# One-core attention-plus-MLP layer: values stored in 64-column groups, a reordered start, and a different cut of the last output tile

## Chip, core and metric

The kernel runs on one core of one Trainium2 chip. The metric is the device time of one execution in microseconds (us). The kernel before takes 269.57 us, the median of three runs (269.50 to 269.68).

The engines are named as in the profile: PE is the matrix engine, PEld its weight loads, DVE the vector engine, ACT the scalar (activation) engine, POOL the general-purpose vector engine, SP the engine whose queue issues most DMAs. PE writes to PSUM (8 banks of 512 f32 columns); the other operands lie in SBUF.

## What is computed

For x of 2048 tokens by 640 features (cut to what matters):

```python
xn = layernorm(x)                                  # per token, eps 1e-5
q, k, v = split(xn @ wqkv)                         # 32 heads of 20
phi(t) = concat(softmax(t @ w_phi), softmax(-(t @ w_phi)))   # 40 features a head
kv = einsum("sf,sd->fd", phi(k), v); z = phi(k).sum(0)       # per head
attn = (phi(q) @ kv) / (phi(q) @ z + 1e-6)         # linear attention
out = x + attn @ wo + (silu(xn @ w1) * (xn @ w3)) @ w2       # F = 1536
```

## The kernel before

**Tiles.** The tokens are 16 tiles of 128 rows (`T`). A tile is normalized in place in `x_tok`, transposed into `xnT` (features on partitions, 5 chunks of 128), and all projections take `xnT` from there. Tiles 0 to 3 are transposed on PE (`xn_transpose`, 5 transposes each, then a copy from PSUM by ACT or DVE); the later ones by DMA transposes.

**Stages, as PE sees them.** (1) Warm-up matmuls on zeros (`idle`, `warm_up`), the transposes of tiles 0 to 3 and their value projections (`v_part`: two halves q of 320 columns, 5 matmuls each, then one copy to `v2` on ACT, `v_store`). (2) The first MLP chunks (`mlp`: 10 matmuls of 512 columns for one chunk of 128 hidden features and 512 tokens) and `fold_mm`, which folds `w_phi` into the key and query weights. (3) Keys and values tile by tile (`k_tile`, `v_tile`). ACT takes exponentials into `ekt`, DVE sums them, POOL divides (`k_norm`, two POOL instructions a tile). (4) `kv_sum`: for each tile 11 groups of three heads, one matmul a group, 63 moving columns (3 heads of 20 values and a one), 42 in the last group, accumulated over the 16 tiles in PSUM. (5) Queries (`q_proj` to `q_tok`), with MLP chunks as filling. `q_tok` has 11 matmuls of 63 columns a tile as well, whose moving operand `KVc` lies in groups of 64 columns. (6) The remaining MLP chunks and the outputs, `out_tile`: 17 chunks accumulate into a 128 by 640 result, DVE adds x, a DMA on SP's queue stores it.

**Values.** `v2` holds, for each tile, 32 heads of 21 bf16 columns (20 values and a one), 672 columns in all. Group g of `kv_sum` starts at column 63 g, that is at byte 126 g of the tile's 1344 bytes. The ones are written by one POOL memset in `consts_late`.

**The order.** The order on each engine is not written out: `_Program` records operations, and a planner at the end of the kernel asks 14 streams (`norms`, `transposes`, `fold_k`, `attention`, `k_norms`, ...) for their next step and commits the one that can start first by a cost model. A stream holds back with `yield None` until counters in `done` are reached. Dependencies are found by granules of SBUF, `GRAN` = 32 bytes (line 23): two operations that touch one granule are ordered, on the same engine too (the second waits for the first one's semaphore). PSUM is tracked by bank.

**The start.** `first_loads` issues on SP and ACT: x tile 0 in two halves, x tile 1, x tile 2, the two halves of the value weights `wv`, x tile 3, then MLP weights. The statistics of tiles 0, 2 and 3 are two `bn_stats` (`ln_half`), a `bn_aggr`, an add of eps on DVE and a power of -1/2 on POOL (`ln_rstd`). Those of tile 1 are two sums by ACT with the mean, eps step and power in between (`act_sum`, `scalar_op`, `act_rstd`). `ln_apply` normalizes on DVE. `norms` gives the order of all this.

**The end.** Tile 15's output is made in two column parts, 0 to 384 and 384 to 640, each with 17 matmuls, one DVE addition and one DMA on SP's queue, so that the first part's addition and store run beside the second part's matmuls (lines 699 to 706).

Of the kernel before, what the change touches and what calls it, by code (L numbers as in the profile page):

```python
# [9 lines left out]
D = 640  # L10
# [9 lines left out]
DEN_EPS = 1e-6  # L20

ENGINES = ("PE", "ACT", "DVE", "POOL", "SP")
GRAN = 32


def heads_of_chunk(c):
# [223 lines left out]
def bass_parallel_sum__linear_kernel_hedgehog__glu_gated_swiglu__prompt_kernel(  # L250
# [11 lines left out]
    bf = DT.bfloat16  # L262
    LAG = 4.0
    QLEAD = 2
    IDLE1, IDLE2 = 11, 8
    f32 = DT.float32
    P = _Program(nc)

# [18 lines left out]
    GM = new("GM", [128, DC, H], bf)  # L287
    phi_s = new("phi_s", [128, DC, DH], bf)
    BDc = new("BDc", [128, DC, 8 * DH], bf)
    bst = new("bst", [128, T, 16], f32)  # L290
    mv = new("mv", [128, T, 8], f32)
    rstd = new("rstd", [128, T, 8], f32)
    mhalf = new("mhalf", [128, 4], f32)
    warm = new("warm", [128, 8], f32)
    M3 = new("M3", [128, 4], bf)
# [28 lines left out]
    eqT = [new(f"eqT{i}", [128, NG, 128], bf, (RKV, RE + 27648)[i // 2] + 5632 + 2816 * (i % 2)) for i in range(4)]  # L324
    hT = [hT0, hT1, hT2, hT3]

    RV = region(21504)
    v2 = new("v2", [128, T, H * 21], bf, RV)
    oT = new("oT", [128, DC, S], bf, RV)

    RW = region(12800)
# [59 lines left out]
    def memset(eng, o, v):  # L391
        P.op(eng, "memset", [o], [], (o, v), cost=0.15 + free(o) / 960)
# [52 lines left out]
    def consts_late():  # L445
        memset("POOL", M3[:, 0:3], 1.0)
        select(M3[:, 0:3], 0, [[-40, 3]], 1, ALU.is_ge, 0.0)
        select(M3[:, 0:3], 40, [[40, 3]], -1, ALU.is_gt, 0.0)
        memset("POOL", ekt[:, T * 2 * D:T * 2 * D + 48], 1.0)
        memset("POOL", v2[:].rearrange("p t (h c) -> p t h c", c=21)[:, :, :, DH], 1.0)  # L450


    def ln_half(t, q):
        i, o = x_tok[:, t, 320 * q:320 * q + 320], bst[:, t, 6 * q:6 * q + 6]
# [49 lines left out]
                 cost=0.9)  # L504

    def warm_up():
        idle(7, 512)
        idle(IDLE1, 128)

    def idle(n, cols):  # L510
        z = t1[:, 2, :]
        for _ in range(n):
            mm(bank(7, cols), z[:, 0:128], z[:, 0:cols], True, True, cost=cols / 1200)

    def xn_transpose(t, k):
        dst = xnT[:, :, t * 128:(t + 1) * 128]
# [30 lines left out]
        evac(dst[:, dc, :].rearrange("p (b c) -> p b c", c=320), bank2(k, 320))  # L547


    def proj(t, w, k):  # L550
        for q in range(2):
            for i in range(DC):
                mm(bank(k + q, 320), xnT[:, i, t * 128:(t + 1) * 128],
                   w[:, i, 320 * q:320 * q + 320], i == 0, i == DC - 1)

    def v_part(t, q, i, k):
        mm(bank(k + q, 320), xnT[:, i, t * 128:(t + 1) * 128], wv[:, i, 320 * q:320 * q + 320],
           i == 0, i == DC - 1)

    def v_store(t, k):  # L560
        pv = bank2(k, 320).rearrange("p b (h c) -> p b h c", c=DH)
        act(v2[:, t, :].rearrange("p (b h c) -> p b h c", b=2, c=21)[:, :, :, 0:DH], pv, ACT.Copy)

    def v_tile(t, k):
        proj(t, wv, k)
        v_store(t, k)

    def k_tile(t, k):
# [15 lines left out]
    def group(g):  # L584
        return 3 * g, min(3, H - 3 * g)

    def at_group(k, g, n):
        return bank(k + g // 8, n, 64 * (g % 8))

    def kv_sum(t0, t1, k):  # L590
        for t in range(t0, t1):
            for g in range(NG):
                h, nh = group(g)
                w = t * 2 * D + 120 * g
                mm(at_group(k, g, 21 * nh), ekt[:, w:w + 128], v2[:, t, 21 * h:21 * (h + nh)],
                   t == 0 and g % 8 == 0, t == T - 1 and g in (7, NG - 1), True, 0.03)

    def kv_store(k):
# [94 lines left out]
    def out_tile(t, k):  # L693
        b, ti = divmod(t, 4)
        if t + 2 < T:
            load_xres(t + 2)
        chunks = [(oT[:, i, t * 128:(t + 1) * 128], wo_s, i) for i in range(DC)]
        chunks += [(hT[b][:, i, ti * 128:(ti + 1) * 128], w2_s, i) for i in range(FC)]
        if t == T - 1:
            for q, lo, hi in ((0, 0, 384), (1, 384, D)):  # L700
                for n, (l, w, i) in enumerate(chunks):
                    mm(bank(k + q, hi - lo), l, w[:, i, lo:hi], n == 0, n == len(chunks) - 1)
                r = xres[:, t % 4, lo:hi]
                tt("DVE", r, bank(k + q, hi - lo), r, ALU.add)
# [19 lines left out]
    done = dict.fromkeys(("w", "ln", "t", "f", "k", "n", "kv", "v", "u", "qp", "qn", "qd", "q", "o", "h"), 0)  # L724

    def norms():
        yield lambda: (first_loads(), consts())
        yield lambda: act_sum(1, ACT.Copy, bst[:, 1, 0:1])
        yield lambda: (ln_half(0, 0), ln_half(0, 1), ln_rstd(0, 1))
        yield lambda: scalar_op(1, mv[:, 1, 0:1], bst[:, 1, 0:1], -1.0 / D, 0.0)  # L730
        yield lambda: act_sum(1, ACT.Square, mv[:, 1, 1:2], mv[:, 1, 0:1])
        yield lambda: ln_apply(0)
        done["ln"] = 1
        yield lambda: act_rstd(1)
        yield lambda: ln_half(2, 0)
        while done["t"] < 1:
# [12 lines left out]
        todo = []  # L749
        for t in range(4, T + 2, 2):  # L750
            if t == T or t > done["k"] + 8:
                for u in todo:
                    yield lambda u=u: ln_apply(u)
                    done["ln"] = u + 1
                todo = []
            if t == T:
                break
            while t > done["k"] + 8:
                yield None
            yield lambda t=t: ln_stats(t, 2)  # L760
# [47 lines left out]
    def attention():  # L808
        def v(t):
            return lambda: v_tile(t, banks(2))  # L810

        yield warm_up
        for t in range(4):
            while done["t"] <= t:
                yield None
            k = banks(2)
            held.add(k // 2)
            for q in range(2):
                for i in range(DC):
                    yield lambda t=t, q=q, i=i, k=k: v_part(t, q, i, k)  # L820
# [197 lines left out]
```

## Time and profile before

| | |
|---|---|
| median of three runs | 269.57 us |
| the profiled execution | 269.42 us |
| its span, first to last instruction | 267.7 us |
| PE busy | 262.3 us, 98% |
| DVE, POOL, ACT busy | 171.3, 103.0, 99.5 us |
| granted PE clock | 1.0 |

Times within the profile count from the start of the span. A row of the timeline gives start, duration, engine, line, operation, output<-input, shape and how many instructions are merged (x5); in brackets is the idle time of the engine before and what ended it. A matmul's duration contains its way through the array, so that matmuls overlap: how fast PE works is read from the distance of their starts, that is (duration of the row - duration of one matmul) / (count - 1). A few matmul records are missing from a trace (here 464 of 480 of one kind): a hole that is just one matmul wide is such a record and no stall. Most operations have line 102, the helper that records them, so tiles tell them apart. The DMA view gives, for each issue, the median time from issue to landing.

### The profile page before, as it was taken

The page shows a single profiled execution, that of the slowest core. Times are in us where ns is not written, and L with a number is a line of the kernel's source. Part 1 is how long each engine was busy: PE and PEld are TensorE (multiplying, and loading weights), DVE is VectorE, ACT ScalarE, POOL GpSimd, SP SyncE. Part 2 cuts the span into 40 slices and gives each one's busy share as a digit, 9 for nine tenths or more (in the row PEclk, how much of TensorE's full clock was granted, in tenths as well). Part 3 has the DMA queues.
Part 4 walks back from the last instruction along what each step waited for, and adds up shares of the span by engine and source line. Part 5 has one row for each costly group of instructions (what it writes and reads, how often), then busy time and mean ns, then how long its engine had stood idle before and what let it go on. Part 6 is the DMA issues. An engine that isn't in the chain of part 4 may idle for free.

```text
span 267.7 us, 4797 instructions
## 1 busy us (share of the span) xinstructions
PE 262.3 (98%) x1943; PEld 160.9 (60%) x1962; DVE 171.3 (64%) x292; ACT 99.5 (37%) x193; POOL 103.0 (38%) x144
## 2 busy tenths in 40 slices
PE   7999999999999999999999999999999999999996
PEld 4656677776745545554455455444577777777774
DVE  4559899998886878888888887898512121212112
ACT  5557979988324443334442344322100000000000
POOL 4316748999996364444444444420000000000000
PEclk9999999999999999999999999999999999999999
DMA  7998695900093444555474464214212213131301
GB/s 223 279 322 155 148 220 109 309 12 2 2 326 73 78 78 81 97 100 95 78 88 95 78 82 78 44 38 78 49 51 74 75 55 94 51 98 49 95 30 49
DMA packets 63510, 27.73 MB, mean 104 GB/s; under 512 B 49792, under 2 KB 63488, under 8 KB 63488
## 3 DMA queue, kind: packets, MB, share of 16 engines
q1 hardware_dynamic: 62688, 26.94, 43.4%
q10 hardware_dynamic: 800, 0.49, 0.6%
q8 instruction: 15, 0.25, 0.4%
q14 instruction: 7, 0.06, 0.1%
HBM read 12.81 MB, written 2.62 MB: 58 GB/s over the span
## 4 chain that ended last, share of the span: by engine, by line
PE 96%; DMA 1%; ACT 1%; issue 1%; DVE 0%; POOL 0%; SPq 0%
PE PS L102 96%; DMA x_tok<-in_A_x_dram 1%; ACT t L102 1%; POOL rstd L102 0%; DVE x_tok L102 0%; DVE xres L102 0%; SPq L114 0%; DVE rstd L102 0%; DVE mv L102 0%
## 5 line engine op out<-in xcount | busy, mean ns | idle before, releaser
L102 PE MATMUL PS<-xnT,w_s 128*128 128x512 bf16 x464 | 105.7, 379 | 1.0 <-ACT Wkp L102 0.2
L102 PEld LDWEIGHTS PS<-xnT,w_s 128*128 128x128 bf16 x480 | 45.8, 98 | 51.3 <-ACT Wkp L102 0.2
L102 PE MATMUL PS<-w_s,hT 128*128 128x320 bf16 (+2 forms) x384 | 54.9, 299 | 0.0
L102 DVE TENSOR_TENSOR xres<-PS,xres 128x640 bf16<-128x640 f32 (+2 forms) x17 | 13.4, 785 | 60.0 <-PE PS L102 60.0
L102 ACT ACTIVATE th<-PS 128x512 f32<-128x512 f32 x48 | 28.8, 600 | 49.0 <-PE PS L102 49.0
L102 PEld LDWEIGHTS PS<-w_s,hT 128*128 128x128 bf16 x384 | 37.6, 98 | 14.6
L102 DVE SCALAR_TENSOR_TENSOR t<-th,PS 128x512 bf16<-128x512 f32 x48 | 32.4, 675 | 20.8 <-ACT th L102 20.8
L102 POOL TENSOR_TENSOR ekt<-ekt,rS 128x640 bf16<-128x640 bf16 x32 | 39.5, 1277 | 0.6 <-DVE rS L102 0.6
L102 ACT ACTIVATE eq<-PS 128x600 bf16<-128x600 f32 (+1 forms) x72 | 24.7, 411 | 29.6 <-PE PS L102 29.5
L102 DVE SCALAR_TENSOR_TENSOR hT<-t,PS 128x512 bf16<-128x512 bf16 x48 | 33.0, 687 | 1.7
L102 PE MATMUL PS<-wv,xnT 128*128 128x320 bf16 x160 | 24.7, 299 | 0.1
L102 PE MATMUL PS<-wo_s,oT 128*128 128x320 bf16 (+2 forms) x160 | 24.5, 299 | 0.0
L102 PE MATMUL PS<-Wkp,xnT 128*128 128x320 bf16 x160 | 23.9, 299 | 0.0
L102 ACT ACTIVATE ekt<-PS 128x640 bf16<-128x640 f32 x32 | 22.3, 703 | 3.8 <-PE PS L102 3.3
L102 PE MATMUL PS<-Wqp,xnT 128*128 128x128 bf16 (+1 forms) x157 | 23.5, 297 | 0.2
L102 POOL TENSOR_TENSOR eq<-eq,rq 128x600 bf16<-128x600 bf16 (+1 forms) x32 | 22.6, 728 | 1.3
L102 DVE TENSOR_REDUCE S<-ekt 128x64 f32<-128x1280 bf16 x16 | 23.0, 1438 | 0.0
L102 POOL TENSOR_TENSOR rq<-rq,Sq 128x32 f32<-128x32 f32 x16 | 4.0, 253 | 48.5 <-DVE rq L102 48.5
L102 POOL TENSOR_TENSOR half<-eq 128x660 f32<-128x660 bf16 x15 | 20.4, 1359 | 3.6 <-ACT eq L102 3.6
L102 PEld LDWEIGHTS PS<-wo_s,oT 128*128 128x128 bf16 x160 | 15.7, 98 | 6.3
L102 PEld LDWEIGHTS PS<-wv,xnT 128*128 128x128 bf16 x160 | 15.3, 98 | 6.5 <-ACT xnT L102 0.5
L102 PEld LDWEIGHTS PS<-Wqp,xnT 128*128 128x128 bf16 x160 | 12.9, 98 | 10.5
(56 smaller groups left out, 182.7 us busy)
## 6 DMA issues: line engine op xcount, KB each, us to landing
w_s<-in_B_w_dram SPq DMA_DIRECT2D x6, 640.0 KB, 6.2
xres<-in_A_x_dram SPq DMA_DIRECT2D x16, 160.0 KB, 2.4
out_dram<-xres SPq DMA_DIRECT2D x15, 160.0 KB, 1.8
x_tok<-in_A_x_dram SPq DMA_DIRECT2D x3, 640.0 KB, 6.4
w_s<-in_B_w_dram SPq DMA_DIRECT2D x1, 1920.0 KB, 8.0
wo_s<-in_A_wo_dram SPq DMA_DIRECT2D x1, 800.0 KB, 8.5
x_tok<-in_A_x_dram SPq DMA_DIRECT2D x3, 160.0 KB, 4.1
wv<-in_A_wqkv_dram ACTq DMA_DIRECT2D x1, 400.0 KB, 4.3
```

The costliest lines, as they stand in the source:

```text
L102: o = _Op(eng, lambda: m(*args, **kw), r, w, cost)
```

## The change

1. `v2` goes from 32 heads of 21 columns to 11 groups of 64 columns (3 heads of 21 and one unused column; 1408 bytes a tile). A value projection writes its two halves into adjoining PSUM columns (192 to 512 of one bank, 0 to 320 of the next), so that `v_store` copies 11 groups of 60 columns in one instruction; 20 of these columns are not part of the product. `kv_sum` reads its moving operand from column 64 g.
2. To make room, `bst`, `mv` and `rstd` are packed to 12, 2 and 2 floats a tile, and `GRAN` becomes 8 bytes. The memset of the ones has 176 groups of 3 elements in place of 512.
3. Warm-up: 8 matmuls of 512 columns, each into a bank of its own, and 7 of 128, in place of 7 and 11 into one bank.
4. Tile 1's transposes stand behind the five matmuls of tile 0's first value half; the second half waits for them.
5. Tile 2's two `bn_stats` stand around tile 1's eps step: one directly ahead of it, one ahead of tile 1's `ln_apply`. (Before, the first stood behind the eps step and the second behind `ln_apply`.)
6. The last tile's parts are 512 and 128 columns; the second part's DMA is issued from ACT's queue.

```diff
-GRAN = 32
+GRAN = 8
-    IDLE1, IDLE2 = 11, 8
+    IDLE1, IDLE2 = 7, 8
-    bst = new("bst", [128, T, 16], f32)
-    mv = new("mv", [128, T, 8], f32)
-    rstd = new("rstd", [128, T, 8], f32)
+    bst = new("bst", [128, T, 12], f32)
+    mv = new("mv", [128, T, 2], f32)
+    rstd = new("rstd", [128, T, 2], f32)
-    RV = region(21504)
-    v2 = new("v2", [128, T, H * 21], bf, RV)
+    RV = region(T * NG * 128)
+    v2 = new("v2", [128, T, NG * 64], bf, RV)
-        memset("POOL", v2[:].rearrange("p t (h c) -> p t h c", c=21)[:, :, :, DH], 1.0)
+        memset("POOL", v_heads(v2[:].rearrange("p t n -> p (t n)"))[:, :, :, DH], 1.0)
+    def v_heads(a):
+        return a.rearrange("p (g x) -> p g x", x=64)[:, :, 0:63].rearrange("p g (h c) -> p g h c", c=21)
     def warm_up():
-        idle(7, 512)
+        idle(8, 512)
...
+            j = 7 - i if cols == 512 else 7
+            mm(bank(j, cols), z[:, 0:128], z[:, 0:cols], True, True, cost=cols / 1200)
...
+    def part(w, t, q, i, k, off=0):
+        mm(bank(k + q, 320, 0 if q else off), xnT[:, i, t * 128:(t + 1) * 128], w[:, i, 320 * q:320 * q + 320],
+           i == 0, i == DC - 1)
...
     def v_store(t, k):
-        pv = bank2(k, 320).rearrange("p b (h c) -> p b h c", c=DH)
-        act(v2[:, t, :].rearrange("p (b h c) -> p b h c", b=2, c=21)[:, :, :, 0:DH], pv, ACT.Copy)
+        pv = PS[:, k * 512 + 192:k * 512 + 192 + 60 * NG].rearrange("p (g h c) -> p g h c", h=3, c=DH)
+        act(v_heads(v2[:, t, :])[:, :, :, 0:DH], pv, ACT.Copy)
...
-                mm(at_group(k, g, 21 * nh), ekt[:, w:w + 128], v2[:, t, 21 * h:21 * (h + nh)],
+                mm(at_group(k, g, 21 * nh), ekt[:, w:w + 128], v2[:, t, 64 * g:64 * g + 21 * nh],
...
-            for q, lo, hi in ((0, 0, 384), (1, 384, D)):
+            for q, lo, hi in ((0, 0, 512), (1, 512, D)):
...
-                finish.append(P.dma("SP", out_t[:, t, lo:hi], r))
+                finish.append(P.dma(("SP", "ACT")[q], out_t[:, t, lo:hi], r))
...
     def norms():
...
+        yield lambda: ln_half(2, 0)
         yield lambda: act_rstd(1)
-        yield lambda: ln_half(2, 0)
         while done["t"] < 1:
             yield None
+        yield lambda: ln_half(2, 1)
         yield lambda: ln_apply(1)
         done["ln"] = 2
-        yield lambda: ln_half(2, 1)
...
     def transposes():
         for t in range(4):
+            while t == 1 and done["v0"] < DC:
+                yield None
...
     def attention():
...
+                    if t == 0 and q == 1:
+                        while done["t"] < 2:
+                            yield None
+                    yield lambda t=t, q=q, i=i, k=k: part(wv, t, q, i, k, 192)
+                    done["v0"] += 1
```

The planner's costs and the changed streams shift the order elsewhere too. Up to the first 12 tiles of `kv_sum` PE's order is the same but for the start. Then the last four tiles of `kv_sum` stand behind 30 MLP matmuls instead of 40, and two query projections come later among the MLP chunks. Towards the end of the queries the order is the same again. On DVE the second `bn_stats` of a tile no longer waits for the first one's semaphore, since the two no longer share a granule. On POOL the memset of `KVc` moves ahead of the first query's scaling. SP's DMAs keep their order; the last store moves to ACT.

More of the change, by code (lines that the diff above doesn't have):

```diff
@@ L511, in idle @@
         z = t1[:, 2, :]
-        for _ in range(n):
-            mm(bank(7, cols), z[:, 0:128], z[:, 0:cols], True, True, cost=cols / 1200)
+        for i in range(n):
+            j = 7 - i if cols == 512 else 7
+            mm(bank(j, cols), z[:, 0:128], z[:, 0:cols], True, True, cost=cols / 1200)
     def xn_transpose(t, k):
@@ L547, in fold_mm, with proj @@
         evac(dst[:, dc, :].rearrange("p (b c) -> p b c", c=320), bank2(k, 320))
-    def proj(t, w, k):
+    def part(w, t, q, i, k, off=0):
+        mm(bank(k + q, 320, 0 if q else off), xnT[:, i, t * 128:(t + 1) * 128], w[:, i, 320 * q:320 * q + 320],
+           i == 0, i == DC - 1)
+    def proj(t, w, k, off=0):
         for q in range(2):
             for i in range(DC):
[L553 to L558, printed above, removed]
+                part(w, t, q, i, k, off)
     def v_store(t, k):
-        pv = bank2(k, 320).rearrange("p b (h c) -> p b h c", c=DH)
-        act(v2[:, t, :].rearrange("p (b h c) -> p b h c", b=2, c=21)[:, :, :, 0:DH], pv, ACT.Copy)
+        pv = PS[:, k * 512 + 192:k * 512 + 192 + 60 * NG].rearrange("p (g h c) -> p g h c", h=3, c=DH)
+        act(v_heads(v2[:, t, :])[:, :, :, 0:DH], pv, ACT.Copy)
     def v_tile(t, k):
-        proj(t, wv, k)
+        proj(t, wv, k, 192)
         v_store(t, k)
@@ L592, in kv_sum @@
             for g in range(NG):
-                h, nh = group(g)
+                nh = group(g)[1]
                 w = t * 2 * D + 120 * g
-                mm(at_group(k, g, 21 * nh), ekt[:, w:w + 128], v2[:, t, 21 * h:21 * (h + nh)],
+                mm(at_group(k, g, 21 * nh), ekt[:, w:w + 128], v2[:, t, 64 * g:64 * g + 21 * nh],
                    t == 0 and g % 8 == 0, t == T - 1 and g in (7, NG - 1), True, 0.03)
@@ L722, in banks @@
         return min((k for k in range(0, 8, n) if k // 2 not in held), key=free_at)
-    done = dict.fromkeys(("w", "ln", "t", "f", "k", "n", "kv", "v", "u", "qp", "qn", "qd", "q", "o", "h"), 0)
+    done = dict.fromkeys(("w", "ln", "t", "f", "k", "n", "kv", "v", "u", "qp", "qn", "qd", "q", "o", "h", "v0"), 0)
     def norms():
@@ L819, in attention @@
                 for i in range(DC):
-                    yield lambda t=t, q=q, i=i, k=k: v_part(t, q, i, k)
+                    if t == 0 and q == 1:
[3 more added lines that the diff above has]
+                    done["v0"] += 1
             yield lambda t=t, k=k: v_store(t, k)
```

## Prediction, before the changed kernel had run

> **What bounds the kernel now.** The page first: the span, the busy times and the chain of work that ended last.
>
> ```profile
> span 267.7 us, 4797 instructions
> ...
> PE 262.3 (98%) x1943; PEld 160.9 (60%) x1962; DVE 171.3 (64%) x292; ACT 99.5 (37%) x193; POOL 103.0 (38%) x144
> ...
> PE 96%; DMA 1%; ACT 1%; issue 1%; DVE 0%; POOL 0%; SPq 0%
> ```
>
> PE is busy for 262.3 of 267.7 us and holds 96% of the chain; the rest of the chain lies at the start (first loads, statistics) and the end (last addition and store). Then the waits, for PE alone, all that the view lists:
>
> ```profile
> PE PS L102 <- DVE warm L102: 1.3, 1, 1.3
> PE PS L102 <- DVE x_tok L102: 0.3, 2, 0.2
> PE PS L102 <- ACT Wkp L102: 0.2, 1, 0.2
> ```
>
> Past the start no wait but one of 0.2 us is left. So an edit pays only where it (a) removes waiting of PE at the start, (b) makes matmuls themselves shorter, or (c) shortens what follows the last matmul. Whatever DVE, ACT or POOL gain elsewhere is worth nothing. All sums below go against the profiled execution, 269.42 us; the median of the runs is 0.15 above it, at 269.57.
>
> **The start (edits 3, 4, 5 and the granules).** PE in the timeline of the first 14 us, and the mean duration of an MLP matmul (379 ns) from the groups:
>
> ```profile
> 6.71 0.45 PE L102 MATMUL PS<-wv,xnT 128*128 128x320 bf16 x2
> 7.31 0.45 PE L102 MATMUL PS<-ident,x_tok 128*128 128x128 bf16 x5 [0.15 <-DVE x_tok L102]
> 7.60 0.84 PE L102 MATMUL PS<-wv,xnT 128*128 128x320 bf16 x5
> 9.25 0.45 PE L102 MATMUL PS<-ident,x_tok 128*128 128x128 bf16 x5
> 12.36 1.53 PE L102 MATMUL PS<-wv,xnT 128*128 128x320 bf16 x10
> 13.94 4.26 PE L102 MATMUL PS<-xnT,w_s 128*128 128x512 bf16 x19
> ...
> L102 PE MATMUL PS<-xnT,w_s 128*128 128x512 bf16 x464 | 105.7, 379 | 1.0 <-ACT Wkp L102 0.2
> ```
>
> Value matmuls start (1.53 - 0.84)/5 = 0.14 us apart (0.136 = 320 columns at the 0.42 ns a column of the MLP's row: its 19 starts span 4.26 - 0.38, 0.216 each); five transposes need 7.60 - 7.31 = 0.29. The last value block ends its issue at 12.36 + 10 x 0.136 = 13.72; the next row starts one 512-column step later, a missing record (19 of 20), so the MLP starts at 13.73. From 6.71 the work is 40 x 0.136 + 3 x 0.29 = 6.31, which ends at 13.02: 0.7 us is waiting, 0.32 of it ahead of tile 1's transposes (6.99 to 7.31). What feeds PE:
>
> ```profile
> 3.14 1.02 DVE L102 BATCH_NORM_STATS2 bst<-x_tok 128x6 f32<-128x320 bf16 x2 [1.93 <-DMA x_tok<-in_A_x_dram]
> 25.42 0.89 DVE L102 BATCH_NORM_STATS2 bst<-x_tok 128x6 f32<-128x320 bf16 x2
> 5.97 0.15 DVE L102 TENSOR_SCALAR rstd<-mv 128x1 f32<-128x1 f32 x1 [0.24 <-ACT t L102]
> 6.04 0.48 DVE L102 BATCH_NORM_STATS2 bst<-x_tok 128x6 f32<-128x320 bf16 x1
> 6.21 0.56 POOL L102 TENSOR_TENSOR rstd<-rstd,mhalf 128x1 f32<-128x1 f32 x1 [0.96 <-DVE rstd L102]
> 6.81 0.45 DVE L102 TENSOR_SCALAR x_tok<-x_tok,mv,rstd 128x640 bf16<-128x640 bf16 x1
> 7.80 0.70 ACT L102 ACTIVATE xnT<-PS 128x640 bf16<-128x640 bf16 x1 [1.14 <-PE PS L102]
> 8.18 0.49 DVE L102 BATCH_NORM_STATS2 bst<-x_tok 128x6 f32<-128x320 bf16 x1
> 8.75 0.45 DVE L102 TENSOR_SCALAR x_tok<-x_tok,mv,rstd 128x640 bf16<-128x640 bf16 x1
> 10.69 0.45 DVE L102 TENSOR_SCALAR x_tok<-x_tok,mv,rstd 128x640 bf16<-128x640 bf16 x1 [0.66 <-POOL rstd L102]
> ```
>
> And the loads of x tiles 2 and 3 (issue on SP, then us to landing):
>
> ```profile
> 1.72 0.42 SPq L114 DMA_DIRECT2D x_tok<-in_A_x_dram  x1
> 2.66 0.52 SPq L114 DMA_DIRECT2D x_tok<-in_A_x_dram  x1
> ...
> x_tok<-in_A_x_dram SPq DMA_DIRECT2D x1, 160.0 KB, 4.1
> ...
> x_tok<-in_A_x_dram SPq DMA_DIRECT2D x1, 160.0 KB, 5.5
> ```
>
> Tile 2 lands at 1.72 + 4.1 = 5.8, tile 3 at 2.66 + 5.5 = 8.16. Now the new order, step by step.
> - Two bn_stats that wait for each other start 1.02 - 0.49 = 0.53 apart, two that don't 0.89 - 0.49 = 0.40. So tile 0 comes 0.12 earlier and its value half starts at about 6.60.
> - Tile 2's first bn_stats now stands ahead of tile 1's eps step. It waits for the landing, starts at 5.82, and eps follows at 6.22 instead of 5.97: 0.25 late. Queued behind it are DVE's half of tile 0's copy (6.29 to 6.56, in time for the fourth value matmul at 7.0) and the other bn_stats (6.49, hidden beside POOL's power). Tile 1 is normalized at 7.06, its transposes start at 7.56.
> - PE issues five value matmuls from 6.60 to 7.29, waits 0.27, transposes tile 1 by 7.85, issues the second half by 8.53. Tile 1's copy on ACT starts 7.80 - 7.31 = 0.49 after the transposes, 8.05, and ends at 8.75; PE goes on at 8.81 with one matmul, to 8.95.
> - Tile 2's aggregate can follow tile 1's normalization at once (7.06 + 0.36, the distance of 6.81 and the row after it), where it had another bn_stats ahead of it; its eps and power end some 0.25 earlier than before and would allow 8.5. But DVE's next instruction, tile 3's bn_stats, waits for the landing at 8.16 as before; 0.40 later, at 8.58, tile 2 is normalized (8.75 before) and transposed at 9.09 (9.25 before).
> - Then PE has 12 value matmuls: 9.09 + 0.29 + 1.63 = 11.01. Tile 3 is normalized 10.69 - 8.75 = 1.94 after tile 2, at 10.52, and can be transposed at 11.02. After that 0.29 and 17 x 0.136: 13.62. The copies of tiles 2 and 3 end 0.49 + 0.70 after the start of their transposes, by 10.3 and 12.2, when PE still has the previous tile's matmuls (to 10.6 and 12.3).
>
> So the MLP starts at 13.62 instead of 13.73: **-0.11**. Most of the waiting is not removed but moved, for the landing of tile 3 (8.16) is late next. Everything to about 68 us has PE's order of before and follows PE. Bounds: +0.15 if tile 2's landing or POOL comes 0.25 later than here, -0.25 if both tile copies come early.
>
> **kv_sum (edit 1).** The old values start at byte 126 g, the new ones at 128 g; the row to compare with is q_tok, also 63 columns a matmul, whose operand already lies in groups of 64:
>
> ```profile
> 68.72 4.25 PE L102 MATMUL PS<-v,ekt 128*128 128x63 bf16 x132
> 81.45 1.52 PE L102 MATMUL PS<-v,ekt 128*128 128x63 bf16 x44
> 87.68 0.48 PE L102 MATMUL PS<-KVc,eqT 128*128 128x63 bf16 x11
> ...
> L102 PE MATMUL PS<-KVc,eqT 128*128 128x63 bf16 x176 | 7.7, 193 | 0.0
> ```
>
> The first kind starts (4.25 - 1.52)/(132 - 44) = 31.0 ns apart; the second, with the last matmul's 0.193 taken off, (0.48 - 0.193)/10 = 29 ns. 176 x 2.0 = **-0.35** on PE, where nothing hides it. Bounds: 0 (start of the operand without effect) and -0.5 (28 ns). The Trainium skill (TensorE: Matmul & The Clock Gate, section "Back-to-back issue gap") gives the distance of warm matmuls as columns/2.4 plus 2.5 ns, whatever the operand's start; by it this term is 0. The trace speaks against it: two rows of 63 columns differ by 2 ns.
>
> ```profile
> L102 ACT ACTIVATE v<-PS 128x640 bf16<-128x640 f32 x16 | 11.2, 701 | 2.4 <-PE PS L102 2.3
> ```
>
> v_store copies 660 columns instead of 640, at 701 ns so far: some 22 ns more each, on an engine that waits for PE ahead of it: nothing. The memset on POOL grows from 512 to 528 elements: nothing, if by elements (see the rivals).
>
> **The end (edit 6).** PE has 17 x 640 columns either way, at 0.42 ns each; matmuls of 128 columns, like the transposes, cost 0.058 instead of 0.054, so 0.07 more at most. The addition and the stores:
>
> ```profile
> 263.37 0.56 DVE L102 TENSOR_TENSOR xres<-PS,xres 128x384 bf16<-128x384 f32 x1 [1.94 <-PE PS L102]
> 265.23 0.42 DVE L102 TENSOR_TENSOR xres<-PS,xres 128x256 bf16<-128x256 f32 x1 [1.30 <-PE PS L102]
> ...
> out_dram<-xres SPq DMA_DIRECT2D x1, 96.0 KB, 1.6
> ...
> out_dram<-xres SPq DMA_DIRECT2D x1, 64.0 KB, 1.5
> ...
> x_tok<-in_A_x_dram ACTq DMA_DIRECT2D x1, 80.0 KB, 2.5
> x_tok<-in_A_x_dram SPq DMA_DIRECT2D x1, 80.0 KB, 2.3
> ```
>
> 128 columns fewer are 0.56 - 0.42 = 0.13 in the addition: 0.29 remains. 32 KB fewer are 0.1 in the store. Against that, ACT's queue landed 0.2 later than SP's for equal loads at the start. The larger part ends 17 x 128 x 0.42 ns = 0.91 later; its addition runs from 264.28 to 264.97 (0.56 + 0.13) and its 128 KB store lands 1.7 later, at 266.7, ahead of the last one. I take **-0.15**, between 0 and -0.23. The Trainium skill (DMA: Bandwidth & Descriptors, section "Specifications") has stores below 512 B a row read back and rewritten; rows of the last part are 256 B. By it the 0.1 in the store is not gained and the term is -0.1; no run here shows such a store.
>
> **Sum.** -0.11 - 0.35 - 0.15 = -0.61: 268.81 for the profiled execution, 268.96 beside the median.
>
> **Rivals.**
> - *The last tile of kv_sum waits for POOL (slower).* The rows:
>
> ```profile
> 25.64 2.37 POOL L102 MEMSET v<- 128x512 bf16 x1
> 42.67 36.91 POOL L102 TENSOR_TENSOR ekt<-ekt,rS 128x640 bf16<-128x640 bf16 x30 [0.59 <-DVE rS L102]
> ```
>
> POOL divides without a pause until 79.58; before, tile 15's matmuls came at 81.45 + 33 x 0.031 = 82.5, 2.9 us later. After, ten MLP matmuls (2.16) move behind: 68.61 + 132 x 0.029 + 30 x 0.216 + 33 x 0.029 = 79.9, with the half of the tile that comes last 0.15 later. Slack 0.4 or so. The memset of the ones stands ahead of POOL's chain. Should its 176 x 3 pattern cost double, POOL ends 2.4 later, PE waits 2.0, and the time is 269.57 - 0.61 + 2.0 = 271.0. It decides from a delay of POOL of 0.4 on, and makes the kernel slower by 0.2% from 1.55. Against it: 16 elements more in 512, and the chain's other inputs move with PE.
> - *The operand's start costs nothing* (the 2 ns come from the weights, which start at byte 240 g before and after): kv_sum 0, 269.3.
> - *The start gains nothing*: the moved waits add up to the old ones, or tile 2 lands later and eps with it: 269.07, with up to 0.15 more.
> - *The end gains nothing*: ACT's queue and the short rows eat 0.15: 269.1.
>
> **How the numbers follow.** A measurement of this kernel tells about 0.2% (0.54 us) from no change, that is, below 269.03. Forecast 0.75, at 268.95; it lies just past the border, and by the bounds of its terms about 0.7 of it, 0.52, is faster and 0.23 the same. The last three rivals together 0.17: same. POOL's wait 0.08: slower. Range: down to all terms at their large ends (-0.25 - 0.5 - 0.23 = -0.98, 268.6), up to kv_sum unchanged and the start 0.15 late, with the end's gain (269.5); it leaves out the POOL case.
>
> **What would show it.** Right: the first MLP matmul near 13.6; kv_sum's first 132 in about 4.0 us instead of 4.25; the last addition near 0.29 us and its store landing within 1.5. Wrong: a wait of PE for POOL ekt near 80 us; kv_sum still 31 ns apart; transposes of tile 2 later than 9.25; any wait of PE between 20 and 260 us.

## The result and the profile after

The changed kernel takes 268.75 us, the median of 22 runs (268.44 to 269.95), the kernel before 269.49 in the 22 runs beside it (269.32 to 269.87). The ratio is 0.9974 with a 95% interval of 0.9968 to 0.9981: **faster by 0.26%, 0.74 us**. The forecast was 268.95, faster, with a range of 268.6 to 269.5. The profiled execution took 268.63 us; 269.42 less 268.63 is 0.79.

The page of the changed kernel: the span and the busy times.

```profile
span 266.9 us, 4814 instructions
...
PE 263.2 (99%) x1959; PEld 159.9 (60%) x1959; DVE 169.9 (64%) x292; ACT 98.0 (37%) x193; POOL 102.9 (39%) x144
```

The span is 0.8 shorter, as the time is. PE's busy time is 0.9 longer, which is no sign of more work: every matmul is on record here (1959 of 1959, before 1943 of 1962), and the lacking ones were not counted as busy. Comparing the two figures would give the wrong sign.

Of PE's waits the view lists only the first, 1.3 us for the warm-up's zeros, as before. Before, it also listed 0.3 for normalized tiles and 0.2 for the folded key weights. That last one was no wait:

```profile
20.14 2.11 PE L102 MATMUL PS<-xnT,w_s 128*128 128x512 bf16 x9 [0.23 <-ACT Wkp L102]
```

This row has 9 of its 10 matmuls and starts one 512-column step (0.216) behind the end of the 30 folding matmuls (18.04 + 1.87 = 19.91), so the hole is a missing record. In the changed kernel all 10 are on record and follow without a break. From the first MLP matmul to the first one of `kv_sum` it is 55.0 us before and after.

A short wait can be missing from the list too (the two found below are), so the start is read from PE's timeline:

```profile
6.66 0.85 PE L102 MATMUL PS<-wv,xnT 128*128 128x320 bf16 x5
7.52 0.45 PE L102 MATMUL PS<-ident,x_tok 128*128 128x128 bf16 x5
7.81 1.27 PE L102 MATMUL PS<-wv,xnT 128*128 128x320 bf16 x6
8.94 0.45 PE L102 MATMUL PS<-ident,x_tok 128*128 128x128 bf16 x5
...
10.89 0.45 PE L102 MATMUL PS<-ident,x_tok 128*128 128x128 bf16 x5
11.18 2.47 PE L102 MATMUL PS<-wv,xnT 128*128 128x320 bf16 x17
13.49 1.89 PE L102 MATMUL PS<-xnT,w_s 128*128 128x512 bf16 x8
```

The last value block runs through, 11.18 + 17 x 0.136 = 13.49, where the MLP starts: 0.24 before the old 13.73. Tile 1's transposes come 0.21 later than before (7.52 for 7.31), tile 2's 0.31 earlier (8.94 for 9.25), tile 3's 0.44 earlier. Two waits are left: 0.18 ahead of tile 1's transposes (five value matmuls from 6.66 end their issue at 7.34), and 0.28 inside the row of 7.81, where the sixth matmul waits for tile 1's copy. The chain of waits, cut to the same stretch (start, duration, what), says the same: PE, then ACT's copy of tile 1, then PE without a break.

```profile
7.52 0.47 PE PS L102 x5
...
8.01 0.71 ACT xnT L102
...
8.77 10.90 PE PS L102 x90
```

DVE's timeline of that time, then POOL's power for tile 2:

```profile
8.04 0.49 DVE L102 BATCH_NORM_STATS2 bst<-x_tok 128x6 f32<-128x320 bf16 x1 [0.27 <-DMA x_tok<-in_A_x_dram]
8.45 0.43 DVE L102 TENSOR_SCALAR x_tok<-x_tok,mv,rstd 128x640 bf16<-128x640 bf16 x1
...
10.38 0.45 DVE L102 TENSOR_SCALAR x_tok<-x_tok,mv,rstd 128x640 bf16<-128x640 bf16 x1 [0.66 <-POOL rstd L102]
...
7.85 0.55 POOL L102 TENSOR_TENSOR rstd<-rstd,mhalf 128x1 f32<-128x1 f32 x1 [0.87 <-DVE rstd L102]
```

Tile 3's first bn_stats waits for its load and starts at 8.04, against 8.18 before; the normalizations of tiles 2 and 3 follow at 8.45 and 10.38. POOL's power for tile 2 ends at 8.40, so two paths meet at 8.45: tile 3's load with the bn_stats behind it (8.04 + 0.40), and tile 2's own statistics.

`kv_sum` and the end, PE's rows and DVE's last addition:

```profile
68.48 3.96 PE L102 MATMUL PS<-v,ekt 128*128 128x63 bf16 x132
78.76 1.43 PE L102 MATMUL PS<-v,ekt 128*128 128x63 bf16 x44
...
264.60 0.29 DVE L102 TENSOR_TENSOR xres<-PS,xres 128x128 bf16<-128x128 f32 x1 [0.26 <-PE PS L102]
```

The matmuls start (3.96 - 1.43)/88 = 28.75 ns apart on average (31.0 before): 176 x 2.25 = 0.40 less. The last addition takes 0.29 for 0.42. Its end stands 2.0 us ahead of the span's end (264.89 of 266.9), as before (265.65 of 267.7): the smaller store itself brings at most 0.05. So the three terms are -0.24, -0.40 and -0.13 to -0.16, together the -0.8 of the span.

POOL's divisions:

```profile
41.13 36.91 POOL L102 TENSOR_TENSOR ekt<-ekt,rS 128x640 bf16<-128x640 bf16 x30 [0.60 <-DVE rS L102]
```

They end at 78.04, 1.5 us earlier than before (79.58); `kv_sum`'s last tile starts at 78.76 + 33 x 0.0288 = 79.71 and does not wait.

### The profile page after: what moved, and what is told of

The parts are those of the page before. It is cut to its first block, busy times and chain, and to the rows that moved or that the text cites. A ratio compares the mean times of both kernels' runs of the same rounds, so it can differ in the third digit from the quotient of the medians.

```text
span 266.9 us, 4814 instructions
## 1 busy us (share of the span) xinstructions
PE 263.2 (99%) x1959; PEld 159.9 (60%) x1959; DVE 169.9 (64%) x292; ACT 98.0 (37%) x193; POOL 102.9 (39%) x144
## 4 chain that ended last, share of the span: by engine, by line
PE 98%; ACT 0%; DVE 0%; issue 0%
PE PS L102 98%; ACT xnT L102 0%; DVE xres L102 0%; DVE t L102 0%; DVE warm L102 0%
## 5 line engine op out<-in xcount | busy, mean ns | idle before, releaser
L102 PE MATMUL PS<-xnT,w_s 128*128 128x512 bf16 x480 | 107.7, 379 | 0.0
L102 ACT ACTIVATE th<-PS 128x512 f32<-128x512 f32 x48 | 29.3, 611 | 49.4 <-PE PS L102 49.4
L102 ACT ACTIVATE eq<-PS 128x600 bf16<-128x600 f32 (+1 forms) x72 | 23.8, 424 | 29.7 <-PE PS L102 29.7
L102 PE MATMUL PS<-Wqp,xnT 128*128 128x512 bf16 (+1 forms) x160 | 24.2, 299 | 0.0
L102 ACT ACTIVATE ekt<-PS 128x640 bf16<-128x640 f32 x32 | 20.6, 709 | 4.8 <-PE PS L102 4.8
```

The lines of the kernel that those rows point to most:

```text
L102: o = _Op(eng, lambda: m(*args, **kw), r, w, cost)
```

## Experiments

The theory after the result: `kv_sum` gains because each group's moving operand now starts on a multiple of 16 bytes; the start gains by the new order of statistics, and by more than forecast because the load of tile 3 came earlier in this execution (the profiles below show that this is half of it: where tile 3 is early enough, tile 2's load decides); the end gains what the shorter addition saves. Rivals: the granules do part of it; the 64-column stride or the weights matter, not where the operand starts; the order of PE (edit 4) makes the start; POOL's chain is a danger close by.

**The change in steps.** Four kernels, timed on one chip against the same runs of the kernel before (269.36 there). The first has one edit on the old kernel:

```diff
-GRAN = 32
+GRAN = 8
```

The second is the changed kernel without edits 4, 5 and 6 (values in groups of 64 columns, packed statistics and new warm-up stay), the third the changed kernel with the old cut of the last tile, and the fourth the changed kernel itself. The cut in the third:

```diff
-            for q, lo, hi in ((0, 0, 512), (1, 512, D)):
+            for q, lo, hi in ((0, 0, 384), (1, 384, D)):
...
-                finish.append(P.dma(("SP", "ACT")[q], out_t[:, t, lo:hi], r))
+                finish.append(P.dma("SP", out_t[:, t, lo:hi], r))
```

> The kernel before with the dependency granules of 8 bytes alone (and the planner's order that follows from them, with the last four tiles of kv_sum 10 MLP matmuls earlier). Theory: only DVE and POOL off the path get earlier, PE's work and its waits stay; 0 to -0.05 us, a ratio of 0.9998 to 1.0. The last division on POOL ends near 78.0 instead of 79.6. Rival (the granules carry part of the gain, by an earlier DVE): -0.2 us or more, with the first MLP matmul before 13.6.

> Granules, packed statistics, the warm-up over eight banks and the values in groups of 64 columns; the start's order and the last tile as before. Theory: kv_sum starts 28.8 ns apart instead of 31.0, 176 x 2.2 = -0.39 us on PE, and nothing else: 0.9985 to 0.9987 of the time before. Rival (part of the 0.8 us comes with the smaller tiles or the warm-up): over -0.5 us. Rival (what kv_sum gains is lost elsewhere): within 0.1 us of before.

> As the run with the values in groups of 64, plus the new order of the start (tile 1's transposes behind tile 0's first value half, tile 2's statistics around tile 1's eps); the last tile as before. Theory: another -0.1 us from the order alone and up to -0.25 us where x tile 3 lands early; in this profile the first MLP matmul stands 5.47 us after the landing of x tile 3, wherever that is between 8.0 and 8.2. Rival (the order itself is worth 0.24 us): 13.5 even with a landing at 8.15. In all -0.5 to -0.63 us, 0.9977 to 0.9981.

> The changed kernel once more, for its spread and its landings. Theory: -0.65 to -0.8 us, 0.9970 to 0.9976; 0.16 us less than the run without the new last tile (0.13 in the addition, 0.03 in the store). Rival: the end gains nothing, and the run equals the one without it.

| kernel | us | ratio, 95% |
|---|---|---|
| granules of 8 bytes alone | 269.33 | 0.9997 (0.9988 to 1.0006) |
| + values in groups of 64, packing, warm-up | 269.03 | 0.9984 (0.9975 to 0.9993) |
| + the new start (edits 4, 5) | 268.78 | 0.9980 (0.9970 to 0.9990) |
| + the new end = the changed kernel | 268.77 | 0.9977 (0.9968 to 0.9987) |

The granules bring nothing to the time. By the medians the values bring 0.30 and the start 0.25, by the ratios 0.35 and 0.11. An interval of 0.1% to either side is 0.27 us, so these times alone do not separate neighbouring steps; the end, expected at 0.16, shows as 0.01 and 0.08. The profiles separate them. One profile of each kernel, in us:

| kernel | first MLP matmul | from it to the end of the span |
|---|---|---|
| before | 13.73 | 253.97 |
| granules | 13.67 | 253.95 |
| + values | 13.85 | 253.58 |
| + start | 13.46 | 253.59 |
| + end, two runs | 13.49, 13.40 | 253.41, 253.41 |

Behind the first MLP matmul the values are worth 0.37 and the end 0.17 to 0.18, and neither the granules nor the start matter there. What lies ahead of that matmul is the start, and it differs from one execution to the next with the loads. The granules alone, on PE, then POOL, then DVE:

```profile
11.55 2.28 PE L102 MATMUL PS<-wv,xnT 128*128 128x320 bf16 x14
68.66 4.25 PE L102 MATMUL PS<-v,ekt 128*128 128x63 bf16 x132
79.22 1.52 PE L102 MATMUL PS<-v,ekt 128*128 128x63 bf16 x44
...
41.26 36.92 POOL L102 TENSOR_TENSOR ekt<-ekt,rS 128x640 bf16<-128x640 bf16 x30 [0.60 <-DVE rS L102]
...
7.95 0.48 DVE L102 BATCH_NORM_STATS2 bst<-x_tok 128x6 f32<-128x320 bf16 x1
8.69 0.45 DVE L102 TENSOR_SCALAR x_tok<-x_tok,mv,rstd 128x640 bf16<-128x640 bf16 x1 [0.26 <-POOL rstd L102]
```

`kv_sum` stays 31.0 ns apart. POOL's chain, though, already starts at 41.26 instead of 42.67: this is the granules' doing, and worth nothing, since PE does not wait for it. Tile 3's load came early here (bn_stats at 7.95), yet tile 2 is normalized at 8.69, because POOL's power of tile 2 is late, and the MLP starts at about 13.67 (the matmuls 11.55 + 14 x 0.136 and a wait of 0.2 for tile 3's copy). The old order cannot use an early load of tile 3.

The end, in the third kernel (old cut) and the fourth (new cut), the last addition and, in PE's row, the last value block of the start:

```profile
11.15 2.47 PE L102 MATMUL PS<-wv,xnT 128*128 128x320 bf16 x17
264.57 0.42 DVE L102 TENSOR_TENSOR xres<-PS,xres 128x256 bf16<-128x256 f32 x1 [1.30 <-PE PS L102]
```

```profile
11.09 2.47 PE L102 MATMUL PS<-wv,xnT 128*128 128x320 bf16 x17
264.51 0.29 DVE L102 TENSOR_TENSOR xres<-PS,xres 128x128 bf16<-128x128 f32 x1 [0.26 <-PE PS L102]
```

From the value block to the end of the addition it is 253.84 with the old cut and 253.71 with the new: 0.13, the addition's own difference. The rest of the 0.17, 0.04, lies behind the addition, where the store is.

**Where the operand starts.** Three kernels, the changed one with all values moved by 2, 8 and 16 bytes (SH = 1, 4, 8); nothing else about the matmuls, stride and weights included, differs. For the room, `M3` lies in `mhalf`'s tensor and `warm` on the sums'.

```diff
-    v2 = new("v2", [128, T, NG * 64], bf, RV)
+    v2 = new("v2", [128, T * NG * 64 + 32], bf, RV)
...
-                mm(at_group(k, g, 21 * nh), ekt[:, w:w + 128], v2[:, t, 64 * g:64 * g + 21 * nh],
+                mm(at_group(k, g, 21 * nh), ekt[:, w:w + 128], v2[:, SH + t * NG * 64 + 64 * g:SH + t * NG * 64 + 64 * g + 21 * nh],
```

> The changed kernel with all of the values moved by one bf16 column: groups of 64 columns as before, but each starts 2 bytes behind a multiple of 128. Theory (what counts is that the moving operand starts on a 16-byte boundary: in the kernel before, only groups 0 and 8, at bytes 0 and 1008, started their successor after 28 ns, the others after 31 to 34): all groups are slow, some 32 ns apart, kv_sum's first 132 matmuls take 4.3 us instead of 3.96. Rival (a group of 64 columns is enough, wherever it starts): 28.8 ns.

> The same with a move of 8 bytes. Theory of 16 bytes: slow as with 2 bytes, about 32 ns. Rival (8 bytes are enough): 28.8 ns.

> The same with a move of 16 bytes. Theory of 16 bytes: 28.8 ns, as in the changed kernel. Rival (32 or 64 bytes are needed): about 32 ns.

PE's timeline, moved by 2 bytes, by 8, by 16:

```profile
68.26 4.06 PE L102 MATMUL PS<-v,ekt 128*128 128x63 bf16 x132
78.63 1.46 PE L102 MATMUL PS<-v,ekt 128*128 128x63 bf16 x44
```

```profile
68.18 4.27 PE L102 MATMUL PS<-v,ekt 128*128 128x63 bf16 x132
78.77 1.53 PE L102 MATMUL PS<-v,ekt 128*128 128x63 bf16 x44
```

```profile
68.24 3.96 PE L102 MATMUL PS<-v,ekt 128*128 128x63 bf16 x132
78.52 1.43 PE L102 MATMUL PS<-v,ekt 128*128 128x63 bf16 x44
```

The distances are (4.06 - 1.46)/88 = 29.5, (4.27 - 1.53)/88 = 31.1 and 28.75 ns. Eight bytes take away the whole gain, sixteen take nothing: it is the start of the operand, with 16 bytes as the unit, and neither the stride nor the weights. Each kernel ran once (268.54, 268.74, 268.39), and the changed kernel's own runs spread wider than that. From the first MLP matmul to the end of the span, though, they take 253.55, 253.83 and 253.41: 8 bytes cost 0.42, where 176 x 2.4 ns is 0.42, and 2 bytes 0.14. Two bytes cost only a third, where the expectation had the full price, so an equal price for every start off the multiple of 16 is not what these rows show.

The starts of single matmuls, averaged over the 16 tiles, show more. In the kernel before, each of groups 1 to 7 and group 9, at every even offset from 2 to 14, starts its successor after 31.5 to 32.9 ns, group 8 (offset 0) after 28.1. With all groups 8 bytes off, group 8 takes 30.9; group 0, however, takes 28.4 there as well, so it is fast without an aligned start. It follows the short group 10. From byte 8 the 126 bytes touch nine blocks of 16, from byte 0 or 2 eight. That would explain 8 and 16, but not why 2 costs anything, nor group 7 of the kernel before, which takes 31.9 at offset 2 with eight blocks. How the price comes about stays open. The Trainium skill (Advanced Engine Details and Errata, section "SBUF Cachelines") has lines of 16 bytes in SBUF and a penalty for changing lines. The unit agrees with 31.1 against 28.75; the intermediate 29.5 it doesn't explain.

**The queue of the last store.** The changed kernel with the last part's DMA back on SP's queue:

```diff
-                finish.append(P.dma(("SP", "ACT")[q], out_t[:, t, lo:hi], r))
+                finish.append(P.dma("SP", out_t[:, t, lo:hi], r))
```

> The changed kernel with the last store (32 KB, rows of 256 bytes) on SP's queue instead of ACT's. Theory: SP has long issued the larger part's store (0.55 us earlier, 0.33 us of issue), so the queue changes little: the last store lands within 0.1 us of the 1.5 after the end of the addition. Rival (ACT's queue costs 0.2 us, as the first loads suggest): it lands 0.2 us earlier, 1.3 after the addition.

The one execution took 268.67. The DMA view's row of the last store, of this kernel, then of the changed one:

```profile
out_dram<-xres SPq DMA_DIRECT2D x1, 32.0 KB, 1.5
```

```profile
out_dram<-xres ACTq DMA_DIRECT2D x1, 32.0 KB, 1.5
```

The same 1.5 from either queue, and the same as the 64 KB of the old cut. ACT's queue brought nothing and cost nothing.

**The start, edit by edit.** The changed kernel with one edit undone each; in the first, the statistics of tile 2 (edit 5), in the second, tile 1's place behind the value half (edit 4).

```diff
-        yield lambda: ln_half(2, 0)
         yield lambda: act_rstd(1)
+        yield lambda: ln_half(2, 0)
...
-        yield lambda: ln_half(2, 1)
         yield lambda: ln_apply(1)
         done["ln"] = 2
+        yield lambda: ln_half(2, 1)
```

```diff
-            while t == 1 and done["v0"] < DC:
-                yield None
...
-                    if t == 0 and q == 1:
-                        while done["t"] < 2:
-                            yield None
```

> The changed kernel with edit 5 undone: tile 2's two bn_stats stand behind tile 1's eps step and behind tile 1's ln_apply again; edit 4 (tile 1's transposes behind the first value half) stays. Theory (the statistics' order is what makes tile 2 early, edit 4 only rearranges PE): tile 2's normalization falls back to some 1.9 us after tile 1's, its transposes to near 9.25, fewer value matmuls (14 instead of 17) are left behind tile 3's transposes, PE waits for tile 3's copy again (0.2 us), and the MLP starts near 13.73 as in the kernel before: 269.0, 0.24 above the changed kernel, ratio about 0.998. Rival (edit 4 carries the start): the MLP still starts near 13.5, 268.77.

> The changed kernel with edit 4 undone: nothing makes tile 1's transposes stand behind the five value matmuls of tile 0's first half; edit 5 stays. Theory (edit 4 is worth nothing by itself): tile 1's transposes start 1.75 us after the landing of x tile 2 in either order, the MLP 5.97 us after these, near 13.49 for a landing at 5.77: 268.77, as the changed kernel, ratio about 0.9975. Rival (edit 4 carries the start): the MLP starts near 13.73, 269.0.

On one chip (before 269.37): old statistics 268.88, ratio 0.9988 (0.9975 to 1.0002); old place of the transposes 268.56, 0.9968 (0.9956 to 0.9979). PE's timeline with old statistics, then with the old place:

```profile
7.28 0.44 PE L102 MATMUL PS<-ident,x_tok 128*128 128x128 bf16 x5
...
11.47 2.28 PE L102 MATMUL PS<-wv,xnT 128*128 128x320 bf16 x14
13.80 1.46 PE L102 MATMUL PS<-xnT,w_s 128*128 128x512 bf16 x6
```

```profile
7.44 0.45 PE L102 MATMUL PS<-ident,x_tok 128*128 128x128 bf16 x5
...
11.24 2.34 PE L102 MATMUL PS<-wv,xnT 128*128 128x320 bf16 x16
```

With the old place the MLP starts at 11.24 + 16 x 0.136 = 13.42, 5.98 after tile 1's transposes; the changed kernel has 13.49 - 7.52 = 5.97. With old statistics it is 6.30 (13.80 less one lacking record of 0.216, less 7.28), and 11.47 + 14 x 0.136 = 13.37 leaves again the 0.2 of waiting for tile 3's copy: with only 14 matmuls behind tile 3's transposes, PE comes to tile 3 before its copy is done; with 16 or 17 it does not. By the medians the kernel with edit 5 undone is 0.32 slower than the one with edit 4 undone. The two intervals overlap a little, so it is the profiles that settle it. Undoing edit 4 costs nothing: its MLP starts 7.74 after tile 2's first bn_stats (5.68), against 7.70 in the changed kernel (5.79). With edit 5 undone the MLP starts at 13.59, not at the 13.73 expected, but tile 2's load had landed at 5.49; the kernels moved by 2, 8 and 16 bytes, with the new order and a landing at 5.45 to 5.54, start it at 13.18 to 13.26. The theory held: edit 5 carries the start, 0.3 to 0.4 where tile 2 lands that early.

What the new order waits for is read from all seven profiles that have it unchanged. The MLP starts 5.03 to 5.05 after tile 2's normalization in each. The normalization comes behind the later of two: the end of POOL's power for tile 2, and tile 3's first bn_stats, which holds DVE for 0.41.

| kernel | tile 2's first bn_stats | tile 3's first bn_stats | POOL's power ends | tile 2 normalized | MLP |
|---|---|---|---|---|---|
| changed | 5.79 | 8.04 | 8.40 | 8.45 | 13.49 |
| changed, again | 5.55 | 7.89 | 8.32 | 8.35 | 13.40 |
| old cut of the end | 5.74 | 7.98 | 8.38 | 8.42 | 13.46 |
| moved by 2 bytes | 5.50 | 7.82 | 8.11 | 8.23 | 13.26 |
| moved by 8 bytes | 5.48 | 7.38 | 8.10 | 8.13 | 13.18 |
| moved by 16 bytes | 5.56 | 7.53 | 8.17 | 8.20 | 13.24 |
| last store on SP | 5.87 | 7.96 | 8.48 | 8.51 | 13.56 |

Only with 2 bytes does tile 3's load decide; in the changed kernel the two paths end together, and in the other five it is POOL's power, which ends 2.61 to 2.64 after tile 2's first bn_stats (2.77 in the second row) and so goes by tile 2's load. The last row shows it best: tile 3 came earlier than in the first row, tile 2 later, and the MLP later.

**The wait that is left.** The changed kernel with tile 1's copy shared by ACT and DVE, as tile 0's is, and tile 3's statistics behind it (not shown: tile 1's transposes take two PSUM banks, and `fold_k` waits for `block_diag`):

```diff
-        for j, a, b in ((0, 0, 3), (1, 3, DC)) if t == 0 else ((0, 0, DC),):
+        for j, a, b in ((0, 0, 3), (1, 3, DC)) if t < 2 else ((0, 0, DC),):
...
+        while done["t"] < 2:
+            yield None
         yield lambda: ln_half(3, 0)
```

> The changed kernel with tile 1's copy out of PSUM split between ACT (384 columns) and DVE (256), as tile 0's is, so that the wait of PE for that copy (0.28 us at 8.5) goes; tile 3's first bn_stats stands behind it. Theory (that wait is covered by what comes after: tile 2's transposes wait for tile 3's bn_stats on DVE, tile 3's copy is late next): the MLP starts near 13.40, 0.1 earlier than in the changed kernel, 268.68; at most 0.25 earlier if tile 3's copy is not late. Rival (the copy of tile 1 sets the start by its full wait): 0.28 earlier, 13.21, 268.5. A third way: DVE's extra 0.29 delays tile 2's normalization and nothing is gained or 0.1 is lost.

268.71, ratio 0.9972 (0.9962 to 0.9982): not to be told from the changed kernel. PE's timeline:

```profile
6.17 1.02 PE L102 MATMUL PS<-t 128*128 128x128 bf16 x8
7.03 0.85 PE L102 MATMUL PS<-wv,xnT 128*128 128x320 bf16 x5
7.71 0.44 PE L102 MATMUL PS<-ident,x_tok 128*128 128x128 bf16 x5
8.00 1.39 PE L102 MATMUL PS<-wv,xnT 128*128 128x320 bf16 x9
9.29 0.45 PE L102 MATMUL PS<-ident,x_tok 128*128 128x128 bf16 x5
...
11.64 2.28 PE L102 MATMUL PS<-wv,xnT 128*128 128x320 bf16 x14
```

Nine value matmuls now run through behind tile 1 (from 8.00, 9 x 0.136 is 1.22, to 9.22), so the wait of 0.28 is gone. But tile 2's transposes come 1.58 after tile 1's (1.42 in the changed kernel), and with 14 matmuls at the end tile 3's copy is late again. In this profile the MLP starts at 13.76, 0.27 later than in the changed kernel, but PE's first value matmul is 0.37 later too (7.03, see the end of the document). By the times the third way of the expectation, nothing gained, is what happened. No kernel tried is measurably faster than the changed one.

**A delay of POOL.** The changed kernel with the memset of the ones issued twice, the delay by which the slower rival was priced:

```diff
+        P.op("POOL", "memset", [ones], [], (ones, 1.0), cost=0.0)
```

> The changed kernel with the memset of the ones on POOL issued twice (2.45 us more there; the computation is the same). This is the delay by which the prediction priced its slower rival. Theory A, as the prediction had it (the memset stands ahead of POOL's chain of divisions, which follows it with a slack of 0.4 us): the chain ends 2.4 later, PE waits 2.0 us for it near 80 us, 270.8. Theory B (the chain ends late by 2.4, but the slack is about 1.5, since the chain ended at 78.04 in the changed kernel and the last tile's matmuls start at about 79.7): PE waits 0.9, 269.7. Theory C (POOL has 4.6 us of idle time between the memset and the stretch without pauses that starts at 41.1 and is released by DVE): the delay is taken up there, the chain ends at 78.0 as before, 268.77.

269.59, ratio 1.0009 (1.0000 to 1.0017), 0.9 over the changed kernel on the same scale of ratios. By the number it is theory B; by the place it is none of the three. PE's, DVE's, ACT's and POOL's rows:

```profile
36.53 1.57 PE L102 MATMUL PS<-wv,xnT 128*128 128x320 bf16 x10 [0.26 <-DVE t L102]
42.40 1.53 PE L102 MATMUL PS<-wv,xnT 128*128 128x320 bf16 x10 [0.23 <-ACT v L102]
79.52 1.43 PE L102 MATMUL PS<-v,ekt 128*128 128x63 bf16 x44
...
31.42 2.68 DVE L102 TENSOR_SCALAR x_tok<-x_tok,mv,rstd 128x640 bf16<-128x640 bf16 x2 [3.58 <-POOL rstd L102]
...
37.65 0.92 ACT L102 ACTIVATE x_tok<-x_tok,rstd 128x640 bf16<-128x640 bf16 x1 [2.76 <-POOL rstd L102]
...
43.52 36.92 POOL L102 TENSOR_TENSOR ekt<-ekt,rS 128x640 bf16<-128x640 bf16 x30 [0.60 <-DVE rS L102]
```

The chain of divisions is late by the full 2.4 (43.52 for 41.13): POOL's idle times ahead of it are waits for DVE, and DVE itself now waited 3.58 us, until 31.42, for the 1/sigma that POOL delivers behind the memset (1.07, until 29.02, in the changed kernel). So the idle time moved along with the delay and took up none of it: theory C fails. But PE lost its time at 36 and 42 us, where its two rows start 0.42 and 0.39 later behind the row before them than in the changed kernel. At 36 it waited for DVE, whose work behind that normalization is 2.40 late and frees a PSUM bank (`t`, at 35.84 for 33.44). At 42 it waited for ACT, which stood still for 2.76 us ahead of another such normalization (0.24 in the changed kernel), and behind it in ACT's order lie the copies that free PE's banks. From the first MLP matmul to `kv_sum` it is 55.9 instead of 55.0: the whole 0.9 is lost ahead of `kv_sum`. When `kv_sum`'s last tile came, at 79.52 + 33 x 0.0288 = 80.47, the chain had just ended (80.44), because PE was late itself. PE did not wait there.

## Why the prediction was right, point by point

- **What bounds the kernel**: right. PE waits nowhere between 20 us and the end, before or after (the one wait of 0.2 us that the prediction read there is a missing record), and the three places named are where the time came from. What the granules freed on DVE and POOL brought nothing.
- **The start, -0.11 forecast, -0.24 in the profile**: the mechanism was right, one input was off. The step that was off is that DVE's bn_stats of tile 3 "waits for the landing at 8.16 as before": it started at 8.04. From there all went as worked out: normalization 0.41 later (0.40 forecast), tile 3's 1.93 after that (1.94), the MLP 3.11 after that (3.10). The other path, tile 2's power on POOL, was forecast to "allow 8.5" and allowed 8.45, so it became the limit at the same moment. The old kernel had a cause of its own for its 8.75 (a bn_stats between tile 1's normalization and tile 2's aggregate, then POOL's power) and gains nothing from an early load, as the granules' kernel shows. So the new order is worth 0.11 with tile 3 at 8.16, by the prediction's sum (no profile of it has so late a load), and 0.24 with tile 3 at 8.04; with a still earlier one it gains no more, for then tile 2's load decides, as the table above shows. That this profile gained 0.24 and not 0.11 is luck with the loads. The prediction drew a bound for tile 2's landing and took tile 3's as fixed.
- **Edits 4 and 5 as one term**: the order of steps forecast for the two together came true; undoing each showed that edit 5 carries the gain.
- **kv_sum, -0.35 forecast, -0.40 measured**: right, and the rival (the 2 ns come from the weights) fell: 8 bytes more, with the same weights, bring 31.1 ns back. The size was taken from q_tok's 29 ns, where 28.75 came. The formula of the Trainium skill (TensorE: Matmul & The Clock Gate, section "Back-to-back issue gap"), columns/2.4 + 2.5 ns for a single warm gap in isolation, gives 28.75 for 63 columns and has no term for the 2.4 ns that a start at byte 8 costs. That it meets the aligned mean is no proof of it here: the last group of each tile has 42 columns, for which it gives 20, and in the changed kernel the next matmul starts 29.4 ns behind that group on average, as behind the others (28.3 to 29.3). So in this stream the columns alone do not set the distance; what does is open.
- **The end, -0.15 forecast, -0.13 to -0.16 measured**: right in sum. The addition's 0.13 is there; of the 0.1 for the store at most 0.05 is. From the first MLP matmul to the end of the span the new cut is worth 0.17 to 0.18. The 32 KB land 1.5 after the issue, as 64 KB did. That is the result to which the Trainium skill's rule on rows below 512 B led (DMA: Bandwidth & Descriptors, section "Specifications"), but a fixed time of some 1.5 for any small store would give it too, and no run here separates them. The fear of ACT's queue was without ground.
- **The rival of POOL's chain**: right not to be chosen, wrong in its numbers. "The chain's other inputs move with PE" failed: the granules alone let POOL's chain start 1.4 sooner, and all edits together 1.5. On DVE four bn_stats in a row, which no longer wait for each other, take 1.67 instead of 1.94, so DVE delivers earlier, and the slack was 79.71 - 78.04 = 1.67 instead of 0.4. And a delay of 2.4 costs 0.9, not 2.0, at another place: POOL's small steps for the normalizations hold DVE and ACT long before the divisions hold PE.
- **The sum**: -0.61 forecast, -0.79 in the profile, -0.74 by the medians. Of the 0.18 in the profile 0.13 is the start, with its luck of the loads, and 0.05 is `kv_sum`. The medians' 0.13 cannot be split in this way.

## What to carry to other kernels

Let the moving operand of many short matmuls start on multiples of 16 bytes: at 63 columns a start at byte 8 cost 2.4 ns in 31, and padding each group by one column removed it. When an order is changed around loads, work the sum out for the spread of each landing, for the old order as for the new: the load that decides can change, and an order that waits for something else first does not see an early load at all. Where times spread more than a step is worth, measure in the profiles from a mark behind the part that spreads: here from the first MLP matmul on, seven profiles with the same work behind it agree within 0.03 us. An engine's idle time is slack only if what it waits for doesn't wait for that engine.

## What was not expected of the hardware

- The load of x tile 3 varies from one execution to the next, by more than the effects looked for, though the kernels issue the same loads in the same order. Its time from issue to landing in the kernel with values in 64s, then in the one moved by 8 bytes:

```profile
x_tok<-in_A_x_dram SPq DMA_DIRECT2D x1, 160.0 KB, 5.8
```

```profile
x_tok<-in_A_x_dram SPq DMA_DIRECT2D x1, 160.0 KB, 4.6
```

- PE's slow first microseconds end at different times. The eight warm-up matmuls behind tile 0's transposes took 1.02 us in the kernel with the shared copy (row at 6.17 above), at some 0.107 each to the end, and 0.61, at 0.056 each, in the one with old statistics:

```profile
5.96 0.61 PE L102 MATMUL PS<-t 128*128 128x128 bf16 x8
```

  The first value matmul came at 7.03 in the one and at 6.59 in the other. The Trainium skill (TensorE: Matmul & The Clock Gate, section "What's actually happening") has this as a window that runs free of the kernel's start. The two rows agree with it in that the pace changes at another time in each, but they show no cause: the granted clock reads 1.00 throughout in both profiles. Medians, not one profile, decide on an edit of the first 10 us.
- A memset of 176 groups of 3 elements took 2.45 us on POOL where one of 512 took 2.37: its time went by the elements (3% more of both), not by the groups.

```profile
24.85 2.45 POOL L102 MEMSET v<- 128x528 bf16 x1
```
